# One retention-and-gated-MLP kernel on one core: every engine's instructions put into another order by a new table of numbers

## The chip, the cores and the metric

One core of one Trainium2 chip runs the kernel, in one launch. The metric is the device time of one execution in microseconds (us). A kernel is timed in several runs and their median is compared. Its one profiled execution gives the trace from which the rows below come. The five engines each take their instructions strictly in the order in which the program holds them: TensorE (PE, matmuls; PEld are its weight loads), VectorE (DVE), ScalarE (ACT), GpSimd (POOL) and SyncE (SP, which only starts DMAs).

## The reference

For four batches, eight heads, 768 tokens and head width 64, a linear attention with a decaying state is computed, and then a gated projection of its output:

```python
gamma = 1.0 - 2.0 ** (-5.0 - np.arange(H))
for t in range(S):
    state = gamma * state + outer(k[t], v[t])        # per batch and head
    y[t] = (1 / sqrt(D)) * q[t] @ state
x = y, heads side by side                            # (4, 768, 512)
gate = sigmoid(sum over k < 5 of conv_w[k] * x shifted by k)
out = (gate * (x @ w_val)) @ w_out                   # all float32
```

## The kernel before, in words

**Tiling.** The 768 tokens of each batch are cut into 6 chunks of 128, so there are 24 pairs of batch and chunk, numbered g = 0 to 23 with the batch running fastest; g = 4c + b. Each g has one loaded tile `att` (q, k and v; 1 MB from g = 4 on, 768 KB before), in a ring of four buffers: the load of one g (`load`, L198) cannot start before the block that used the buffer four places earlier is through. A load also waits for the fourth-last projection matmul that stands before it in the program (`hold`, L178).

**Attention.** The first four g are done with whole 128-token matmuls (`wide_scores` L263, `turn` L350, `wide_state` L338, `wide_y` L319). From g = 4 on one `block(g)` (L720) holds some 128 small matmuls: the output from this chunk's masked scores (`y_scores`, L360), the state updates (`state`, L240), the output from the state (`y_state`, L360), and the next chunk's scores (`scores`, L219). Around a block, DVE masks the scores (`mask`, L228, tile `u`), ACT copies the state out (`snap`, L250), POOL scales v by the decay (`decay`, L210, writing `att`), and DVE takes the result out to `x` (`evac`, L413).

**Projections.** For every token chunk n = 0 to 5 the four batches together are 512 columns. The value projection (`val(n, m, i)`, L555) is twelve matmuls for each of four column groups m; the output projection (`outp(n, b, i, cs)`, L583) is twelve for each batch b. Float32 precision is had by splitting: each operand is rounded (`xh`, `gvh`, `wvh`, `woh`, on ACT, L422, L571, L524) and its remainder is kept (`xl`, `gvl`, `wvl`, `wol`, on POOL, L426, L575, L528), and three products are summed. The twelve matmuls of one tile keep their order. Their order in `outp` is the one below, so the tenth, eleventh and twelfth need the fourth weight row block of w_out (number 7 of the eight blocks of both weights), rounded and remainder:

```python
ct = i // 3
gvh, gvl = gvs[n, ct]
gg, w = ((gvh, woh), (gvh, wol), (gvl, woh))[i % 3]
```

Results sit in two PSUM banks `mm` in turn; a bank comes free when DVE (`gated`, L564) or ACT (`store`, L593) has read it. The gate's convolution is one ACT and four DVE steps for each tile (`tap`, L539 and L541), then a sigmoid on ACT (L548).

**Weights.** The weights arrive as 64-bit words (`load_w`, L441: eight blocks, number 0 with the small tables as `first_sb`) and are turned into float32 on the chip, in a chain over three engines for each block n: three ACT steps (L465, L469, L473), `cv_bits`, `cv_top`, `cv_exp`, `cv_rest` on DVE (L484, L490, L496, L500), `cv_sum` (L507) on POOL, or on DVE for block 7, then `cv_round` on ACT (L524) and `cv_low` on POOL (L528).

**What sets the order.** Each piece of work is a `Step` with an engine, the tiles that it reads and writes, and a due time. `plan` (L49) sorts the steps by due time, which gives every step a number, and then issues them by the table `TURNS`, a list of those numbers; it only checks that the order respects data and buffers. Negative entries are fillers: -1 a 512-column and -2 a 128-column matmul of zeros (`fill`, L325) that keeps TensorE occupied. So the table alone decides, for each engine, what stands before what:

```python
for step in plan(steps, TURNS, [Step(0.0, "PE", 0.2345, [], [], fill, (n,)) for n in (512, 128)]):
    step.fn(*step.args)
```

Of the kernel before, what the change touches and what calls it, by code (L numbers as in the profile page):

```python
# [91 lines left out]
def tile_retention_gated_mlp(  # L92
# [507 lines left out]
    def first_sigmoid():  # L600
# [28 lines left out]
        12, 6, 5, 1, 2, 13, 11, 4, 0, 20, 15, 17, 14, 19, -2, 28, 8, 29, 7, 18, 10, 46, 59, 60, 21, 53,  # L629
        16, 70, 22, -2, -1, -2, -1, -1, 32, 81, 61, 62, 63, 64, 23, 65, 24, 66, 33, 9, 26, 25, 94, 35,  # L630
        -1, 48, 34, 36, 3, 95, 52, 27, 47, 96, 49, 97, 74, 136, 67, 51, 71, 75, 68, 50, 30, 98, 31, 82,
        69, 72, 99, 54, 116, 84, 100, 106, 55, 58, 79, 107, 101, 57, 108, 73, 83, 56, 109, 80, 78, 110,
        85, 102, 76, 103, 91, 77, 86, 87, 111, 89, 104, 37, 112, 90, 117, 88, 38, 154, 93, 113, 127, 92,
        125, 118, 146, 39, 199, 105, 133, 128, 126, 130, 119, 40, 137, 120, 42, 41, 140, 121, 132, 142,
        -1, 200, 43, 141, 131, 147, 201, 114, 122, 202, 148, 165, 149, 115, 139, 203, 150, 135, 123,
        166, 151, 153, 155, 134, 144, 171, 206, 167, 172, 145, 129, 168, 173, 174, 138, 169, 156, 152,
        -2, 209, 175, 214, 170, 211, 143, 158, 124, 161, 193, 212, 213, 44, 215, 176, 192, 197, 222,
        216, 191, 159, 160, 223, 157, 194, 219, 45, 162, 205, 224, 163, 177, 220, 238, 239, 207, 225,
        281, 178, 196, 282, 283, 195, 269, 198, 284, 240, 241, 204, 164, 244, 179, 287, 226, 246, 218,
        210, 270, 221, 227, 271, 181, 208, 182, 272, 255, 217, 288, 232, 183, 289, 180, 259, 290, 228,  # L640
        318, 260, 261, 184, 229, 262, 319, 263, 230, 316, 273, 231, 322, 185, 236, 274, 266, 248, 186,
        317, 233, 367, 249, 237, 368, 291, 243, 292, 264, 187, 320, 276, 293, 250, 242, 369, 295, 267,
        323, 251, 370, 360, 245, 247, 297, 321, 361, 252, 188, 362, 372, 253, 324, 296, 373, 268, 325,
        277, 374, 326, 254, 327, 328, 329, 275, 300, 256, 375, 376, 363, 377, 279, 378, 189, 330, 301,
        331, 234, 257, 379, 190, 332, 364, 278, 280, 302, 365, 258, 298, 381, 306, 303, 333, 299, 307,
        477, 343, 478, 479, 382, 480, 294, 481, 308, 334, 304, 482, 235, 335, 285, 339, 345, 483, 309,
        346, 348, 305, 310, 383, 336, 311, 371, 484, 385, 366, 398, 452, 399, 485, 312, 386, 400, 502,
        402, 384, 403, 404, 337, 405, 313, 406, 265, 387, 454, 314, 388, 455, 315, 486, 390, 338, 487,
        488, 456, 407, 489, 408, 409, 355, 504, 392, 410, 457, 340, 490, 286, 341, 411, 342, 344, 356,
        347, 380, 391, 349, 350, 413, 462, 463, 393, 464, 414, 458, 465, 351, 563, 352, 353, 354, 506,  # L650
        466, 565, 467, 397, 468, 395, 469, 470, 436, 471, 415, 357, 472, 358, 473, 416, 394, 474, 417,
        418, 419, 448, 420, 451, 434, 450, 401, 421, 460, 422, 423, 424, 425, 498, 426, 435, 427, 389,
        510, 437, 396, 475, 453, 412, 492, 476, 507, 428, 459, 500, 429, 430, 438, 439, 431, 511, 440,
        441, 493, 442, 432, 443, 444, 501, 461, 512, 433, 445, 513, 494, 446, 514, 447, 566, 515, 499,
        517, 519, 666, 567, 667, 668, 491, 669, 568, 670, 671, 672, 495, 673, 569, 516, 674, 675, 496,
        676, 677, 520, 678, 521, 522, 509, 523, 524, 503, 525, 644, 505, 497, 536, 526, 645, 527, 573,
        508, 574, 646, 575, 359, 576, 577, 679, 648, 578, 579, 449, 580, 518, 581, 582, 540, 689, 583,
        584, 543, 690, 545, 585, 546, 547, 529, 548, 586, 549, 550, 649, 553, 587, 554, 588, 589, 555,
        557, 590, 560, 591, 592, 687, 593, 594, 595, 596, 651, 597, 598, 652, 599, 653, 600, 654, 655,
        602, 656, 657, 658, 533, 659, 530, 608, 531, 660, 535, 661, 650, 662, 532, 663, 603, 541, 552,  # L660
        730, 609, 538, 610, 611, 731, 612, 613, 624, 695, 627, 732, 614, 629, 542, 696, 631, 604, 632,
        615, 664, 537, 616, 617, 633, 698, 528, 605, 634, 635, 636, 606, 639, 640, 699, 641, 618, 534,
        642, 619, 544, 607, 688, 680, 620, 681, 621, 539, 559, 700, 682, 637, 558, 736, 665, 737, 556,
        738, 701, 702, 733, 739, 703, 622, 704, 734, 705, 706, 707, 564, 709, 623, 710, 711, 683, 561,
        684, 685, 735, 740, 625, 807, 712, 741, 742, 713, 765, 743, 551, 744, 808, 745, 562, 714, 746,
        601, 792, 793, 715, 747, 794, 795, 748, 796, 797, 766, 799, 818, 819, 800, 767, 801, 802, 803,
# [388 lines left out]
```

## Time and profile before

| | us |
|---|---|
| median of three runs | 211.51 (210.23 to 211.98) |
| the profiled execution | 210.03 |
| its span, first to last instruction | 208.3 |

| engine | busy us | share of the span |
|---|---|---|
| PE | 199.1 | 96% |
| DVE | 136.2 | 65% |
| ACT | 110.3 | 53% |
| POOL | 105.8 | 51% |

The profiled execution is 1.7 us longer than its span, and 1.5 us shorter than the median of the runs. Matmuls are pipelined and overlap, so PE's busy time is not the sum of their durations; the step from one start to the next is what a matmul costs in a dense stretch.

### The profile page before, as it was taken

What the parts mean: (1) busy time and instruction counts of PE and PEld (TensorE: products, weight loads), DVE (VectorE), ACT (ScalarE), POOL (GpSimd) and SP (SyncE); (2) the same over time, 40 slices, a digit from 0 to 9 for tenths busy, and PEclk for the clock granted to TensorE, in tenths of its full rate; (3) what the DMA queues carried; (4) which work ended last, traced back from release to release, by engine and by line L of the source; (5) the groups of instructions that cost most, each with busy time, mean ns of one, the idle gap of its engine ahead of it and who ended that gap; (6) DMA issues with size and microseconds to landing.
All of it is one profiled execution on the core that took longest, in us unless ns stands there. A gap on an engine that the chain in (4) does not pass through costs nothing.

```text
span 208.3 us, 7483 instructions
## 1 busy us (share of the span) xinstructions
PE 199.1 (96%) x3317; PEld 160.4 (77%) x3317; DVE 136.2 (65%) x209; ACT 110.3 (53%) x228; POOL 105.8 (51%) x98
## 2 busy tenths in 40 slices
PE   3999699999999999999999999999999999999993
PEld 2688587786788788787788888788878787877783
DVE  0998999999999592956077888533956457671000
ACT  4577894797486745362665144737060753523321
POOL 2377699899884725934019620295420465132200
PEclk9999999999999999999999999999999999999999
DMA  6999988876463525928104663272010111111122
GB/s 205 389 407 341 344 325 337 307 302 209 127 233 157 178 80 200 385 82 296 53 3 149 260 168 140 89 270 99 9 50 0 50 53 50 50 50 50 50 104 101
DMA packets 8402, 35.18 MB, mean 169 GB/s; under 512 B 937, under 2 KB 1193, under 8 KB 5810
## 3 DMA queue, kind: packets, MB, share of 16 engines
q1 hardware_dynamic: 8352, 34.66, 45.4%
q8 instruction: 26, 0.43, 0.8%
q10 hardware_dynamic: 18, 0.04, 0.3%
q14 instruction: 6, 0.05, 0.1%
HBM read 28.41 MB, written 6.29 MB: 167 GB/s over the span
## 4 chain that ended last, share of the span: by engine, by line
PE 82%; DMA 7%; POOL 4%; ACT 3%; issue 1%; DVE 0%; ACTq 0%; POOLq 0%; SPq 0%
PE mm L583 32%; PE mm L555 29%; PE sy L360 9%; DMA att<-in_att_dram 6%; PE sy L219 4%; PE z_ps L240 3%; POOL xl L426 2%; POOL att L210 1%; PE sy L263 1%; DMA wst<-in_fall_dram 1%; PE mm L350 1%; PE z_ps L325 1%; ACT xh L422 1%; POOL wvl L528 1%; ACT snap L250 1%
## 5 line engine op out<-in xcount | busy, mean ns | idle before, releaser
L541 DVE SCALAR_TENSOR_TENSOR acc<-x,cw_sb,acc 128x512 f32<-128x512 f32 x96 | 70.4, 752 | 5.5 <-ACT acc L539 4.3
L575 POOL TENSOR_TENSOR gvl<-gate,gvh 128x512 fp32r<-128x512 f32 x24 | 31.0, 1296 | 45.9 <-ACT gvh L571 45.9
L426 POOL TENSOR_TENSOR xl<-x,xh 128x512 fp32r<-128x512 f32 x24 | 30.6, 1295 | 21.4 <-ACT xh L422 21.2
L583 PE MATMUL mm<-wol,gvh 128*128 128x512 f32 (+1 forms) x100 | 38.3, 387 | 0.0
L583 PE MATMUL mm<-woh,gvh 128*128 128x512 f32 (+1 forms) x100 | 38.3, 389 | 0.0
L564 DVE TENSOR_TENSOR gate<-mm,gate 128x512 f32<-128x512 f32 x24 | 16.5, 689 | 33.3 <-PE mm L555 20.7
L583 PE MATMUL mm<-woh,gvl 128*128 128x512 f32 (+1 forms) x100 | 38.0, 387 | 0.0
L593 ACT COPY o_sb<-mm 128x512 f32<-128x512 f32 (+1 forms) x25 | 14.2, 571 | 39.7 <-PE mm L583 39.6
L555 PE MATMUL mm<-xh,wvh 128*128 128x512 f32 x96 | 30.7, 408 | 0.3 <-ACT xh L422 0.2
L555 PE MATMUL mm<-xl,wvh 128*128 128x512 f32 x96 | 30.3, 399 | 0.1
L210 POOL TENSOR_TENSOR att<-att,first_sb 128x512 f32<-128x512 f32 x24 | 25.1, 1049 | 9.1 <-DMA att<-in_att_dram 5.6
L555 PE MATMUL mm<-xh,wvl 128*128 128x512 f32 x96 | 29.0, 400 | 0.0
L548 ACT ACTIVATE gate<-acc 128x512 f32<-128x512 f32 x24 | 14.3, 599 | 20.0 <-DVE acc L541 19.3
L583 PEld LDWEIGHTS mm<-woh,gvh 128*128 128x128 f32 x100 | 18.7, 188 | 5.3 <-ACT o_sb L593 1.6
L583 PEld LDWEIGHTS mm<-woh,gvl 128*128 128x128 f32 x100 | 18.8, 188 | 4.0
L583 PEld LDWEIGHTS mm<-wol,gvh 128*128 128x128 f32 x100 | 18.8, 188 | 3.9
L555 PEld LDWEIGHTS mm<-xl,wvh 128*128 128x128 f32 x96 | 17.9, 188 | 4.6 <-POOL xl L426 0.5
L555 PEld LDWEIGHTS mm<-xh,wvh 128*128 128x128 f32 x96 | 17.3, 188 | 5.0 <-ACT xh L422 0.9
L555 PEld LDWEIGHTS mm<-xh,wvl 128*128 128x128 f32 x96 | 17.9, 188 | 4.2
L571 ACT CAST gvh<-gate 128x512 fp32r<-128x512 f32 x24 | 14.8, 619 | 9.5 <-DVE gate L564 7.7
L250 ACT COPY snap<-z_ps 128x256 f32<-128x256 f32 x40 | 14.0, 374 | 9.1 <-PE z_ps L240 6.5
L539 ACT ACTIVATE acc<-x,cw_sb 128x512 f32<-128x512 f32 x24 | 16.5, 695 | 3.8 <-DVE rest L500 3.6
(65 smaller groups left out, 262.2 us busy)
## 6 DMA issues: line engine op xcount, KB each, us to landing
att<-in_att_dram SPq DMA_DIRECT2D x20, 1024.0 KB, 5.7
out_dram<-o_sb SPq DMA_DIRECT2D x23, 256.0 KB, 2.4
wst<-in_w_dram SPq DMA_DIRECT2D x7, 512.0 KB, 7.6
att<-in_att_dram SPq DMA_DIRECT2D x3, 768.0 KB, 8.1
first_sb<-in_first_dram SPq DMA_DIRECT2D x1, 568.0 KB, 4.0
att<-in_att_dram SPq DMA_DIRECT2D x1, 512.0 KB, 4.8
att<-in_att_dram SPq DMA_DIRECT2D x1, 256.0 KB, 8.3
out_dram<-o_sb SPq DMA_DIRECT2D x2, 128.0 KB, 1.8
```

The costliest lines, as they stand in the source:

```text
L210: nc.gpsimd.tensor_tensor(v, v, vd_sb[:, c, :].unsqueeze(2).broadcast_to([P, 8, HALF]), op=ALU.mult)
L250: nc.scalar.copy(sn, z_ps[:, :, b])
L360: return nc.tensor.matmul(sy[cols, h, off:off + HALF], lhsT=lhsT, rhs=rhs, start=start, stop=True, skip_group_check=True,)
L426: nc.gpsimd.tensor_tensor(xl[n, ct], xs[n][:, ct, :, HALO:], xh[n, ct].bitcast(F32), op=ALU.subtract)
L539: nc.scalar.mul(acc, x[:, :, 0:P], cw_sb[:, m, 0:1])
L541: nc.vector.scalar_tensor_tensor(acc, x[:, :, k:k + P], cw_sb[:, m, k:k + 1], acc, op0=ALU.mult, op1=ALU.add,)
L548: nc.scalar.activation(gate[n, m], accs.pop((n, m)), AF.Sigmoid)
L555: products.append(nc.tensor.matmul(vps[n, m], lhsT=w[:, m, ct * P:(ct + 1) * P], rhs=xx[n, ct].rearrange("p b t -> p (b t)"), start=(i == ...
L564: nc.vector.tensor_tensor(gv, vps.pop((n, m)), gv, op=ALU.mult)
L571: nc.scalar.copy(gvs[n, m][0], gate[n, m])
L575: nc.gpsimd.tensor_tensor(gvl, gate.pop((n, m)), gvh.bitcast(F32), op=ALU.subtract)
L583: products.append(nc.tensor.matmul(ops[n, b, cs.start][:, 0:cs.stop - cs.start], lhsT=gg[:, b * P:(b + 1) * P], rhs=w[:, ct, cs], start=(i ...
```

## The change

Only the table `TURNS` changes. The steps, their numbers, the buffers and the holds on loads are the same. The new table has 1219 entries for 1226: the five 512-column and four 128-column fillers become one of each, the 1217 steps are all kept, and the last 321 entries, from step 873 on, are the same in both. A line of the start of each:

```diff
     TURNS = (
-        12, 6, 5, 1, 2, 13, 11, 4, 0, 20, 15, 17, 14, 19, -2, 28, 8, 29, 7, 18, 10, 46, 59, 60, 21, 53,
-        16, 70, 22, -2, -1, -2, -1, -1, 32, 81, 61, 62, 63, 64, 23, 65, 24, 66, 33, 9, 26, 25, 94, 35,
...
+        12, 6, 1, 2, 13, 4, 0, 11, 5, 15, 3, 20, 14, 17, 19, 7, 8, 28, 9, 59, 18, 60, 16, 10, 29, 61,
+        46, 21, 32, 53, 62, 22, 70, 23, 63, 33, 24, 35, 26, 25, 48, 36, 34, 136, 64, 47, 65, 49, 27, 66,
...
```

**SyncE, the first loads.** The first rows after the branch, in the kernel before; a row's size is partitions by 4-byte words, `x2` stands for two alike:

```order
L436 DMA first_sb<-in_first_dram 128x1136
L198 DMA att<-in_att_dram 128x1024
L441 DMA wst<-in_w_dram 128x1024
L198 DMA att<-in_att_dram 128x1536 x2
L198 DMA att<-in_att_dram 128x512
L198 DMA att<-in_att_dram 128x1536
L441 DMA wst<-in_w_dram 128x1024 x2
```

and in the changed one:

```order
L436 DMA first_sb<-in_first_dram 128x1136
L198 DMA att<-in_att_dram 128x1024
L198 DMA att<-in_att_dram 128x1536
L441 DMA wst<-in_w_dram 128x1024
L198 DMA att<-in_att_dram 128x512
L198 DMA att<-in_att_dram 128x1536 x2
L441 DMA wst<-in_w_dram 128x1024 x2
```

The tile of g = 1 now goes third, ahead of weight block 1, and the v of g = 0 (the 512-word row) goes ahead of the tiles of g = 3 and 2. What stands before weight block 3 (the last row's first) is the same set in both. Further on, weight block 6 moves ahead of the load of g = 5, block 4 ahead of that of g = 7, and g = 9 ahead of g = 8.

**VectorE, the last weight block.** Between the mask of g = 11 and the first tap behind the sum of weight block 7, before (`u` is a mask, `gate<-mm` a gating, `x<-sy` an evacuation, `rest<-acc,top` the sum of block 7):

```order
L228 TENSOR_TENSOR u<-sy,tri_sb 128x512
L413 TENSOR_TENSOR x<-sy,dec 128x512
L541 SCALAR_TENSOR_TENSOR acc<-x,cw_sb,acc 128x512
L484 SCALAR_TENSOR_TENSOR acc<-wst,acc 128x512
L490 SCALAR_TENSOR_TENSOR top<-wst,acc 128x512
L564 TENSOR_TENSOR gate<-mm,gate 128x512
L496 TENSOR_SCALAR acc<-top 128x512
L413 TENSOR_TENSOR x<-sy,dec 128x512
L500 SCALAR_TENSOR_TENSOR acc<-wst,acc 128x512
L228 TENSOR_TENSOR u<-sy,tri_sb 128x512
L507 TENSOR_TENSOR rest<-acc,top 128x512
```

and in the changed kernel:

```order
L228 TENSOR_TENSOR u<-sy,tri_sb 128x512
L564 TENSOR_TENSOR gate<-mm,gate 128x512
L490 SCALAR_TENSOR_TENSOR top<-wst,acc 128x512
L413 TENSOR_TENSOR x<-sy,dec 128x512
L496 TENSOR_SCALAR acc<-top 128x512
L500 SCALAR_TENSOR_TENSOR acc<-wst,acc 128x512
L507 TENSOR_TENSOR rest<-acc,top 128x512
L228 TENSOR_TENSOR u<-sy,tri_sb 128x512
```

The evacuation of g = 11 and the mask of g = 12 now stand behind the sum, so two steps fewer are ahead of it; the two rows that are missing above moved ahead of the first.

**TensorE, between block 11 and block 12.** The output products of chunk 0 there, with tile numbers (before, `mm_1166` is batch 3 and `mm_1270` batch 1; gvh_1154 and gvl_1155 belong to the fourth row block):

```order
L583 MATMUL mm_1166<-wol_95,gvh_961 128x512
L583 MATMUL mm_1270<-woh_94,gvh_718 128x512
L583 MATMUL mm_1270<-wol_95,gvh_718 128x512
L583 MATMUL mm_1166<-woh_94,gvl_962 128x512
L583 MATMUL mm_1270<-woh_94,gvl_719 128x512
L583 MATMUL mm_1270<-woh_94,gvh_722 128x512
L583 MATMUL mm_1270<-wol_95,gvh_722 128x512
L583 MATMUL mm_1270<-woh_94,gvl_723 128x512
L583 MATMUL mm_1270<-woh_94,gvh_961 128x512
L583 MATMUL mm_1270<-wol_95,gvh_961 128x512
L360 MATMUL sy_97<-u_1283,att_1076 64x64 x16
```

and after (`mm_1164` is batch 3, `mm_1186` batch 1; gvh_1063 and gvl_1064 belong to the fourth row block), without the first five rows, which are batch 1's products of the second and third row blocks:

```order
L583 MATMUL mm_1186<-woh_94,gvl_958 128x512
L583 MATMUL mm_1186<-woh_94,gvh_1063 128x512
L583 MATMUL mm_1164<-woh_94,gvh_1063 128x512
L583 MATMUL mm_1164<-wol_95,gvh_1063 128x512
L583 MATMUL mm_1164<-woh_94,gvl_1064 128x512
L583 MATMUL mm_1186<-wol_95,gvh_1063 128x512
L583 MATMUL mm_1186<-woh_94,gvl_1064 128x512
L360 MATMUL sy_97<-u_1262,att_1044 64x64 x16
```

The products of the fourth row block, for which weight block 7 must be ready, moved from behind block 12 to ahead of it.

## Rows read from the trace of the kernel before

**Rows 1.** Busy time of each engine in two stretches (us, PE, PEld, DVE, ACT, POOL, PEclk, DMA).

```profile
core 0: us, PE busy (x) PEld busy (x) DVE busy (x) ACT busy (x) POOL busy (x), PEclk, DMA share, GB/s
22.00:57.00 35.00, 32.92 (x914) 25.79 (x910) 34.48 (x56) 25.91 (x56) 31.98 (x27) 1.00 0.75 279
57.00:205.00 148.00, 147.76 (x2187) 119.69 (x2179) 86.06 (x127) 70.08 (x143) 62.04 (x52) 1.00 0.34 120
```

**Rows 2.** Timeline of PE: first product, block 10, two products, the last one.

```profile
22.92 0.73 PE L555 MATMUL mm<-xh,wvh 128*128 128x512 f32 x2 [0.22 <-ACT xh L422]
...
56.59 0.69 PE L360 MATMUL sy<-u,att 64*64 64x64 f32 x32
...
58.61 0.50 PE L555 MATMUL mm<-xl,wvh 128*128 128x512 f32 x1
...
59.41 0.39 PE L583 MATMUL mm<-woh,gvl 128*128 128x512 f32 x1
59.64 0.39 PE L583 MATMUL mm<-woh,gvh 128*128 128x512 f32 x1
...
204.66 0.27 PE L583 MATMUL mm<-woh,gvl 128*128 128x256 f32 x1
```

**Rows 3.** Waits of PE and PEld, 22 to 57 us: total, times, longest.

```profile
PEld sy L360 <- DVE u L228: 1.5, 4, 0.4
PE z_ps L240 <- POOL att L210: 1.2, 3, 0.7
PEld z_ps L240 <- ACT snap L250: 0.9, 2, 0.5
PEld mm L555 <- POOL xl L426: 0.5, 1, 0.5
```

**Rows 4.** Timeline of PE in the first 13 us.

```profile
5.09 1.67 PE L325 MATMUL z_ps<-const-float32-0.0 128*128 128x128 bf16 x5
6.69 2.08 PE L263 MATMUL sy<-att 64*128 64x128 f32 x16
8.70 1.11 PE L350 MATMUL mm<-eye_sb,att 128*128 128x128 f32 x4
...
10.79 1.16 PE L263 MATMUL sy<-att 64*128 64x128 f32 x16
11.88 0.66 PE L350 MATMUL mm<-eye_sb,att 128*128 128x128 f32 x4
```

**Rows 5.** Timeline: weight block 3 reaches ACT and then DVE.

```profile
15.68 0.66 ACT L465 ACTIVATE acc<-wst 128x512 f32<-128x512 f32 x1 [0.72 <-DMA wst<-in_w_dram]
...
17.68 0.70 DVE L484 SCALAR_TENSOR_TENSOR acc<-wst,acc 128x512 int32<-128x512 int32 x1 [0.71 <-ACT acc L473]
```

**Rows 6.** Timeline of DVE up to the sum of weight block 7.

```profile
63.41 0.68 DVE L413 TENSOR_TENSOR x<-sy,dec 128x512 f32<-128x512 f32 x1
64.00 0.68 DVE L500 SCALAR_TENSOR_TENSOR acc<-wst,acc 128x512 f32<-128x512 uint16 x1
64.60 0.68 DVE L228 TENSOR_TENSOR u<-sy,tri_sb 128x512 f32<-128x512 f32 x1
65.20 0.68 DVE L507 TENSOR_TENSOR rest<-acc,top 128x512 f32<-128x512 f32 x1
```

**Rows 7.** Timeline of ACT and POOL: weight block 7 rounded, its remainder.

```profile
65.92 0.62 ACT L524 CAST woh<-rest 128x512 fp32r<-128x512 f32 x1 [0.34 <-DVE rest L507]
...
66.61 1.27 POOL L528 TENSOR_TENSOR wol<-rest,woh 128x512 fp32r<-128x512 f32 x1 [2.81 <-ACT woh L524]
```

**Rows 8.** Timeline of PE: block 12, the products behind it, and block 11's start.

```profile
61.12 0.69 PE L360 MATMUL sy<-u,att 64*64 64x64 f32 x32
...
65.68 0.69 PE L360 MATMUL sy<-u,att 64*64 64x64 f32 x32
...
67.70 0.50 PE L583 MATMUL mm<-woh,gvh 128*128 128x512 f32 x1
68.03 0.41 PE L583 MATMUL mm<-wol,gvh 128*128 128x512 f32 x1
```

**Rows 9.** Timeline of POOL: sum of block 5, remainders of blocks 4 and 5.

```profile
54.48 1.30 POOL L507 TENSOR_TENSOR rest<-rest,top 128x512 f32<-128x512 f32 x1 [0.29 <-DVE rest L500]
56.03 2.53 POOL L528 TENSOR_TENSOR wol<-rest,woh 128x512 fp32r<-128x512 f32 x2 [0.25 <-ACT woh L524]
```

**Rows 10.** Costliest groups of instructions: two of POOL (busy us, mean ns, idle before).

```profile
L575 POOL TENSOR_TENSOR gvl<-gate,gvh 128x512 fp32r<-128x512 f32 x24 | 31.0, 1296 | 45.9 <-ACT gvh L571 45.9
...
L210 POOL TENSOR_TENSOR att<-att,first_sb 128x512 f32<-128x512 f32 x24 | 25.1, 1049 | 9.1 <-DMA att<-in_att_dram 5.6
```

128 rows, old and new, of the table TURNS are left out of this document.

## The prediction, written before the changed kernel had run

> **What bounds the kernel now.** I read first the busy time by stretches [rows 1]. From 57 to 205 us TensorE is busy 147.76 of 148 us: behind 57 us nothing that another engine does can be seen on it, and every step on TensorE simply stands behind the one before. From 22 to 57 us it is VectorE that has no room (34.48 of 35 us), and GpSimd is nearly full too (31.98). So the end of the kernel is set by how much TensorE has done when it becomes dense, and that is set by VectorE and GpSimd.
>
> Next the timeline of TensorE [rows 2]. A product costs 0.23 us (59.41 to 59.64) and a block 2.02 us (56.59 to 58.61). From 22.92 to the start of block 10 at 56.59 the table puts 69 products and six blocks: 69 x 0.23 + 6 x 2.02 = 28.0 us of work in 33.7 us. Some 5.7 us are lost there, and the waits say for what [rows 3]: masks from VectorE, decayed values and remainders from GpSimd, state copies from ScalarE, each a few tenths. A new order can win only from these 5.7 us, from the start before 22.92 us, and nothing from the last matmul at 204.66 us on, since the last 321 entries of the table are the same.
>
> **The start.** Two things change there. The fillers: five ran at 5.09 us for 1.67 us [rows 4], and the first scores came behind them, at 6.69 us; the new table starts the scores as soon as their tile lands. And the loads: the tile of g = 1 goes third and the v of g = 0 comes earlier, so the buffer of g = 0 should come free earlier and with it the load of g = 4. Neither reaches VectorE's full stretch. That one begins with weight block 3: ScalarE waited 0.72 us for its landing (15.68 us), and VectorE 0.71 us for ScalarE (17.68 us) [rows 5]. The same bytes stand ahead of block 3 in both orders, so it lands at the same time, and the same three ScalarE steps (15.68 to 17.68) follow. I take 0 for the start. The bounds: 0.7 us better, VectorE's wait gone, if block 3 lands earlier; 1.5 us worse by the clock (the first rival).
>
> **Weight block 7 and the point where TensorE gets dense.** The longest chain that the new table puts in front of TensorE is that of the last weight block. Before, TensorE reached its remainder behind block 12: the product with `wol` at 68.03 us [rows 8], with the remainder ready at 66.61 + 1.27 = 67.88 us [rows 7], so 0.15 us of room. In the new order the two products with `wol` of row block 7 stand ahead of block 12. What is ready by then can be counted in the table: at the first of these products TensorE has behind it 72 value products, 20 output products and the blocks up to 11. Before, at the start of block 12 (65.68 us [rows 8]) it had the same with 17 output products, so the same amount of work was done at 65.68 + 3 x 0.23 = 66.37 us. That is the mark: the remainder of block 7 before 66.37 us is a gain, behind it a loss, one for one, as all the work that follows is the same and was dense.
>
> When is it ready? The sum of block 7 on VectorE started at 65.20 and took 0.68 [rows 6]. Two steps that stood before it, an evacuation and a mask, now stand behind it; from start to start they took 0.59 us (63.41 to 64.00) and 0.60 us (64.60 to 65.20), together 1.19. The rounding on ScalarE and the remainder on GpSimd follow as before: from the sum's end at 65.88 to 67.88, 2.00 us [rows 6, 7]. At VectorE's old pace that is 65.88 - 1.19 + 2.00 = 66.69 us, 0.32 us late. VectorE was idle 0.52 us between 22 and 57 us [rows 1]; the new order has masks and sums in other places, where I find their inputs earlier, so I give it 0.5 us of that (bounds 0 and 0.5, plus the 0.7 of the start). Then the remainder is there at 66.19 us, and the gain is 0.18 us.
>
> **Does TensorE get there in time?** The three more products by block 10 (72 for 69) and five more by block 11 are work in hand, some 1 us of it, which pays for the waits that the order has anew. The dearest is weight block 5. Its remainder came 4.10 us behind the start of its sum (54.48 to 56.03 + 2.53 = 58.56 us [rows 9]). The new order puts a decay (1.05 us) and a remainder of the gated values (1.30 us) ahead of it [rows 10], and so 6.45 us. At the old pace this is 60.93 us; VectorE's step before the sum stands one place (0.60 us) earlier, and with the 0.5 us from above it is 59.83 us. From there eight products, block 11 and eight products lead to the first product with block 7: 59.83 + 16 x 0.23 + 2.02 = 65.5 us, before 66.19. At the old pace it would be 66.6 us, so this second chain nearly binds as well: 0.2 us late at worst. Hence I take it as hidden; without the cover it costs that 0.2.
>
> **Behind 67 us** the order is new as well up to about 155 us. There TensorE had no wait to lose and VectorE, ScalarE and GpSimd were busy 86, 70 and 62 of 148 us [rows 1], so every new wait is a pure loss and none a gain. I went through the buffers: a decay for g = 21 stands on GpSimd ahead of two remainders of chunk 2, and its load behind a store and the load of g = 19; there some 3 us of room are left by the count of products. I take 0, with 3 us as the upper bound, when one load is late by twice that room.
>
> **Sum.** Start 0, block 7 -0.18, the rest 0: about -0.2 us. The profiled execution of 210.03 us would become 209.8, and the median of the runs, 211.51, 211.3 us. (The profiled one is 1.5 us faster than the median; I forecast the median.)
>
> **Rivals.** (1) The clock at the start; slower. The PEclk column reads 1.00, yet the first sixteen score matmuls took 2.08 us at 6.69 us and the next sixteen 1.16 us at 10.79; four transposes 1.11 and then 0.66 [rows 4]. So TensorE ran at its lower level, 1.2 GHz, until about 10.5 us, and at 2.4 GHz behind. Until then it had been kept occupied from 3.6 us on, by fillers where there was no work. Without them it stands still for about a microsecond before the first scores. If the rise comes later by the second scores, a state and an output (0.92 us for the scores, about as much for the other two together), part of it hides behind the wait for the tile of g = 2 and some 1.5 us reach VectorE. Then block 7 is ready at 67.7 us, 1.3 us behind the mark: 212.8 us. It decides from the point where VectorE's step of block 3 starts later than 17.9 us. Against it: the engine is at work without a pause from about 6.2 us on. The Trainium skill speaks for it (TensorE: Matmul & The Clock Gate, Part 1: The HAM clock gate): the slow clock is the resting state, and only sustained activity lifts it; by that rule alone the missing fillers put the rise off, and the sum would be this rival's.
>
> (2) A new wait behind 67 us, in a stretch that is dense now; 1 to 3 us, so 212.5 to 214.5. For it: everything is reordered and nothing can be won there. Against it: two thirds of the time of VectorE and half of that of the others is free.
>
> (3) Block 7 stops binding. If the loads at the start come earlier by VectorE's 0.71 us of waiting [rows 5] and the 0.5 us hold, the remainder is ready at 65.5 us, when TensorE arrives: a gain of 0.9 us, 210.6. With the waits of the middle shorter too, 2 us: 209.5. For it: 5.7 us are lost in the middle, and the new order does have more products in hand. Against it: VectorE's list up to the sum is the same list less two steps, and it was full.
>
> (4) It does nothing at all: the work of all engines is the same and TensorE's is 96% of the span; then the time is 211.5, which differs from the forecast by less than can be told.
>
> **How the numbers follow.** Forecast and (4), which a measurement cannot part: 0.56. Rival (1) 0.14, (2) 0.12, (3) 0.18. Faster or slower by over 1% means under 209.4 or over 213.6 us, which is about what a measurement of this kernel can tell from no change. Under 209.4 lie half of (3) and a little of the forecast: 0.13. Over 213.6 lie most of (2) and the bad end of (1), with a stall that I did not see: 0.18. The rest, 0.69, is within 1%. The likeliest case alone has 210.6 to 212.1. The range 209.3 to 213.6 leaves out about 1 in 10 on either side.
>
> **What would show it.** Right: VectorE's first step on block 3 within 0.3 us of 17.68; the sum of block 7 ending near 64.2 us; TensorE waiting for `wol` ahead of block 12 and starting that block near 67.1 us, with four more products than the 20 behind it; nothing but tenths of waits behind it. Wrong: sixteen scores at 2 us each still behind 11 us; a gap on TensorE behind 70 us; or block 12 started without a wait.

## The result and the profile after

The changed kernel takes 212.43 us (median of 20 runs, 211.19 to 214.04), the kernel before 211.54 us (20 runs alternating with them, 209.99 to 213.71): 1.0065 of the time before, 95% interval 1.0044 to 1.0086. It is slower, by 0.9 us, where 0.2 us of gain was forecast; the time lies inside the range and within 1%.

The profiled executions lie further apart than the medians: 211.71 us after, 210.03 before. That of before was near the fast end of its runs. Ratios of many runs decide below, and single traces show where a delay sits. A ratio leaves out executions over 1.5% above the fastest of their kernel, so it can differ from the ratio of two medians (run 10 in the table below).

The busy time by stretches of the changed kernel, to be held against [rows 1]:

```profile
core 0: us, PE busy (x) PEld busy (x) DVE busy (x) ACT busy (x) POOL busy (x), PEclk, DMA share, GB/s
22.00:57.00 35.00, 33.95 (x926) 26.50 (x923) 34.52 (x55) 25.86 (x54) 31.55 (x28) 1.00 0.73 267
57.00:205.00 148.00, 147.06 (x2188) 118.41 (x2187) 86.42 (x129) 70.15 (x144) 63.81 (x53) 1.00 0.35 121
```

VectorE is as full from 22 to 57 us as before. Behind 57 us TensorE is idle for 0.94 us in place of 0.24, nearly all of it at block 10 (shown with run 5). Its last matmul, for which [rows 2] have 204.66 us:

```profile
206.38 0.27 PE L583 MATMUL mm<-woh,gvl 128*128 128x256 f32 x1
```

Now the start, on the timeline of TensorE (start, duration, instruction, output and inputs, count, idle time before it and what ended that), against [rows 4]:

```profile
6.10 2.08 PE L263 MATMUL sy<-att 64*128 64x128 f32 x16 [0.92 <-DMA att<-in_att_dram]
8.11 1.11 PE L350 MATMUL mm<-eye_sb,att 128*128 128x128 f32 x4
9.64 1.09 PE L350 MATMUL mm<-eye_sb,att 128*128 128x128 f32 x4 [0.42 <-DMA att<-in_att_dram]
10.65 2.08 PE L263 MATMUL sy<-att 64*128 64x128 f32 x16
```

The second sixteen scores still take 2.08 us (1.16 before): TensorE is at its lower level, 1.2 GHz, behind 10.5 us, though the PEclk column reads 1.00 there as well. Then weight block 3 on ScalarE and VectorE, against [rows 5]:

```profile
16.54 0.67 ACT L465 ACTIVATE acc<-wst 128x512 f32<-128x512 f32 x1 [0.28 <-DMA wst<-in_w_dram]
...
18.54 0.70 DVE L484 SCALAR_TENSOR_TENSOR acc<-wst,acc 128x512 int32<-128x512 int32 x1 [0.49 <-ACT acc L473]
```

Both 0.86 us later than before. And the stretch of weight block 7: its sum on VectorE, its remainder on GpSimd, TensorE at the first product that needs it, and block 12 (against [rows 6 to 8]):

```profile
65.02 0.69 DVE L507 TENSOR_TENSOR rest<-acc,top 128x512 f32<-128x512 f32 x1
...
66.45 1.32 POOL L528 TENSOR_TENSOR wol<-rest,woh 128x512 fp32r<-128x512 f32 x1 [3.75 <-ACT woh L524]
...
67.97 0.40 PE L583 MATMUL mm<-wol,gvh 128*128 128x512 f32 x1
...
68.99 0.69 PE L360 MATMUL sy<-u,att 64*64 64x64 f32 x32
```

The remainder is ready at 67.77 us, and TensorE comes for it at 67.97, without a wait. The prediction's mark for that same point of work was 66.37 us. So TensorE is 1.6 us late there, nearly all of the 1.7 us by which its last matmul is late: the loss is made ahead of 68 us, and weight block 7 does not make it, though by 0.2 us only: had TensorE come earlier than that, it would have waited.

### The profile page after: what moved, and what is told of

The parts are those of the page before. It is cut to its first block, busy times and chain, and to the rows that moved or that the text cites. A ratio compares the mean times of both kernels' runs of the same rounds, so it can differ in the third digit from the quotient of the medians.

```text
span 210.0 us, 7467 instructions
## 1 busy us (share of the span) xinstructions
PE 199.4 (95%) x3310; PEld 160.2 (76%) x3310; DVE 135.7 (65%) x209; ACT 110.6 (53%) x228; POOL 105.5 (50%) x98
## 4 chain that ended last, share of the span: by engine, by line
PE 77%; POOL 6%; DMA 5%; DVE 4%; ACT 4%; issue 2%; SPq 0%; ACTq 0%
PE mm L583 32%; PE mm L555 25%; PE sy L360 7%; DMA att<-in_att_dram 5%; PE sy L219 3%; PE z_ps L240 3%; POOL xl L426 3%; PE sy L263 2%; DVE acc L541 2%; PE mm L319 1%; POOL rest L507 1%; PE z_ps L338 1%; PE mm L350 1%; POOL att L210 1%; ACT acc L465 1%
## 5 line engine op out<-in xcount | busy, mean ns | idle before, releaser
L541 DVE SCALAR_TENSOR_TENSOR acc<-x,cw_sb,acc 128x512 f32<-128x512 f32 x96 | 69.4, 750 | 10.4 <-ACT acc L539 9.4
L555 PE MATMUL mm<-xh,wvh 128*128 128x512 f32 x96 | 31.7, 410 | 0.3 <-ACT xh L422 0.2
L555 PE MATMUL mm<-xl,wvh 128*128 128x512 f32 x96 | 29.6, 400 | 0.1
L228 DVE TENSOR_TENSOR u<-sy,tri_sb 128x512 f32<-128x512 f32 x20 | 13.7, 684 | 7.6 <-PE sy L219 7.5
```

Source lines behind the costliest of these rows:

```text
L541: nc.vector.scalar_tensor_tensor(acc, x[:, :, k:k + P], cw_sb[:, m, k:k + 1], acc, op0=ALU.mult, op1=ALU.add,)
L555: products.append(nc.tensor.matmul(vps[n, m], lhsT=w[:, m, ct * P:(ct + 1) * P], rhs=xx[n, ct].rearrange("p b t -> p (b t)"), start=(i == ...
```

## The experiments

The eighteen kernels differ from the two known ones in the table alone (step numbers in the diffs; 20 is the load of weight block 1, 15 the tile of g = 1, 7 and 8 the position sums, 32 and 48 the first scores and the second transposes). Each was timed in five rounds beside the kernel before; ratios are to that kernel, with 95% intervals. "Changed" means the changed kernel.

### The start: fillers and third load (runs 1 to 4, 8)

Run 1, the fillers back in the changed kernel:

```diff
-17, 19, 7, 8, ... 21, 32, 53, ... 25, 48, 36, ...
+17, 19, -2, 7, 8, ... 21, -2, -1, -2, -1, -1, 32, 53, ... 25, -1, 48, 36, ...
```

> The changed order with the seven early fillers of the kernel before put back at their old places (one 128 ahead of the first matmul; 128, 512, 128, 512, 512 ahead of the first scores; 512 between the two transposes). Theory C (clock): the changed kernel ran its second sixteen scores at 2.08 us because TensorE's clock rose at 14.1 us and not at 10.5; with the fillers the rise is back near 10.5 us, the second scores take 1.16 us, and the time falls from 1.0065 of before to about 0.998. Theory L (third load): weight block 3 still reaches ScalarE at 16.5 us, VectorE's step on it still starts near 18.4 us, and the time stays near 1.005. Theory W (the wait for weight block 7 ahead of block 12 costs by itself): unchanged at 1.0065.

Measured 212.53 us, 1.0062 (1.0033 to 1.0092). The second scores run fast again, yet VectorE comes as late:

```profile
10.48 1.16 PE L263 MATMUL sy<-att 64*128 64x128 f32 x16
...
16.50 0.67 ACT L465 ACTIVATE acc<-wst 128x512 f32<-128x512 f32 x1 [1.84 <-DMA wst<-in_w_dram]
...
18.51 0.70 DVE L484 SCALAR_TENSOR_TENSOR acc<-wst,acc 128x512 int32<-128x512 int32 x1 [0.69 <-ACT acc L473]
```

ScalarE now stands 1.84 us for the landing: the loads alone hold it.

Run 2, weight block 1 third again, no fillers:

```diff
-0, 11, 5, 15, 3, 20, 14,
+0, 11, 5, 20, 15, 3, 14,
```

> The changed order with one load moved: weight block 1 third and the tile of g = 1 fourth, as before. Theory L: weight block 3 lands 0.9 us earlier, ScalarE starts on it at 15.7 us instead of 16.5, and the time falls to about 1.000. Theory C: the clock still rises near 14 us, ScalarE is held by the slow third transpose until 16.2 us anyway, so VectorE's step on block 3 moves by 0.3 us at most and the time stays at 1.005. Theory W: 1.0065.

Measured 213.02 us, 1.0111 (1.0064 to 1.0157). Here the load is in time and the clock is late:

```profile
10.97 2.08 PE L263 MATMUL sy<-att 64*128 64x128 f32 x16
...
16.87 0.64 ACT L465 ACTIVATE acc<-wst 128x512 f32<-128x512 f32 x1
...
18.85 0.70 DVE L484 SCALAR_TENSOR_TENSOR acc<-wst,acc 128x512 int32<-128x512 int32 x1
```

No landing is named ahead of ScalarE's step: its other work, which hangs on TensorE, came late. In these two traces either cause alone makes VectorE 0.8 to 1.2 us late at block 3.

Run 3 has both edits.

> Both: fillers back and weight block 1 third, the rest of the changed order kept. Theories C and L together: VectorE's step on block 3 starts at 17.7 us or earlier as before, the remainder of block 7 is ready near 66.3 us, and the time is 0.998 to 1.000 of before. Theory W: still 1.005 or more, with TensorE waiting ahead of block 12.

VectorE starts block 3 early again, so the start is repaired:

```profile
17.52 0.70 DVE L484 SCALAR_TENSOR_TENSOR acc<-wst,acc 128x512 int32<-128x512 int32 x1 [0.16 <-ACT acc L473]
```

But the time is 212.28 us, 1.0056 (1.0021 to 1.0091): hardly anything comes back. Its profiled execution took 215.8 us, so its trace is not read behind 52 us.

Run 4 takes the first seven fillers out of the kernel before.

```diff
-19, -2, 28, 8, ... 22, -2, -1, -2, -1, -1, 32, ... -1, 48, ...
+19, 28, 8, ... 22, 32, ... 48, ...
```

> The order before without its first seven fillers, nothing else. Theory C: the clock rises near 14 us here too, the second scores take 2.08 us, and the time rises to 1.004 to 1.007 of before. Theory L: the clock does not matter, VectorE's step on block 3 stays at 17.7 us and the time within 0.2% of before. Theory W: no change.

Measured 212.96 us, 1.0084 (1.0046 to 1.0121). So the fillers are worth something; but in this trace the second scores took 1.16 us and VectorE came at 17.95, and the loss that it shows is a wait of GpSimd, 1.73 us ahead of a decay at 36.20. By which path the median loses 0.8% is not shown. The sum over all traces helps with the clock: in the ten with these fillers (before among them) the second scores always took 1.16 us, in the ten without them 2.08 us three times (changed, runs 2 and 6), 1.48 and 1.20 once each, and 1.16 five times. Without fillers the clock's rise is late in some executions only.

Run 8 exchanges the third and the fourth load in the kernel before.

```diff
-0, 20, 15, 17, 14, 19,
+0, 15, 20, 17, 14, 19,
```

> The kernel before with one edit: the tile of g=1 (768 KB) third and weight block 1 (512 KB) fourth, its fillers kept. Theory S in its form L (a larger third load makes every byte behind it late): weight block 3 reaches ScalarE near 16.5 for 15.7, VectorE near 18.5 for 17.7, and the end is 0.8 to 0.9 us later, 212.4 us. If the start's delay is lost in waits that are there anyway: 211.6. If the order of the two loads does not matter to the arrival of block 3: 211.6 with VectorE at 17.7.

Measured 211.46 us beside 210.96, 1.0026 (0.9995 to 1.0057), VectorE at 18.45 us: the arrival as theory L has it, about half its price, with an interval that still holds no change. What the exchange does is seen in the answers on DMA for the third and the fourth load (size, us from issue to landing), before:

```profile
wst<-in_w_dram SPq DMA_DIRECT2D x1, 512.0 KB, 6.1
...
att<-in_att_dram SPq DMA_DIRECT2D x1, 768.0 KB, 6.6
```

and in the changed kernel:

```profile
att<-in_att_dram SPq DMA_DIRECT2D x1, 768.0 KB, 7.8
...
wst<-in_w_dram SPq DMA_DIRECT2D x1, 512.0 KB, 7.6
```

SyncE issues the fourth at 3.16 and 3.22 us, so the same 1.25 MB is in at 9.8 us before and 10.8 after; in run 8, with the exchange alone, at 10.2 (3.11 + 7.1). On the mean it is in at 9.8 us with weight block 1 third (10 traces, 9.5 to 10.2) and at 10.4 with g = 1 third (10 traces, 10.1 to 10.8). Over the traces VectorE starts block 3 at 17.7 us on the mean with weight block 1 third and the fillers in (8 traces, 17.47 to 18.02), at 18.3 with g = 1 third (10 traces, eight of them without the fillers, 17.80 to 18.62): 0.6 us, less than the 0.86 of the first two traces.

### Blocks 10 to 12 (runs 5 to 7)

The trace of the changed kernel has two waits on TensorE at block 10 that the kernel before has not:

```profile
58.47 0.69 PE L360 MATMUL sy<-u,att 64*64 64x64 f32 x32 [0.58 <-DVE x L413]
59.43 0.69 PE L240 MATMUL z_ps<-att 64*64 64x64 f32 x32 [0.26 <-ACT snap L250]
```

Run 5 takes both away: evacuations of g = 9 (275) and 10 (294) on VectorE and the state copy of g = 11 (279) on ScalarE earlier.

```diff
-277, 300, 331, 375, 363, ... 302, 278, 379, 365, 275, ... 303, 279, 280, ... 343, ... 398, 294, 399,
+277, 300, 279, 331, 375, 275, 363, ... 302, 278, 379, 365, ... 303, 280, ... 343, 294, ... 398, 399,
```

> After, with three moves between blocks 9 and 11: on VectorE the evacuation of g=9 ahead of the tap (1,1,3) and the evacuation of g=10 right behind the mask of g=11, on ScalarE the state copy of g=11 right behind the tap (1,0,0); all three as the kernel before has them. Theory M (a second loss, apart from the start: in the changed kernel TensorE waits 0.58 us ahead of block 10 for VectorE's evacuation and 0.26 us inside it for the state copy, and VectorE is held up behind it): block 10 starts at 57.9 for 58.47 with neither wait, 0.84 us come back, 211.7 us. Theory W (the wait for weight block 7 ahead of block 12 is just hidden by those 0.84 us): the product that needs it is reached near 67.1 while the remainder is ready near 67.8 to 68.4, so 0 to 0.2 us come back, 212.3 to 212.5. Theory S (all of the loss is the start's 0.86 us, from the third load and the clock): 212.5.

Measured 213.0 us, 1.0107 (1.0067 to 1.0147): nothing gained. Block 10 starts at 57.38 us without a wait, and half a microsecond is lost inside it instead, for GpSimd's decay:

```profile
58.82 0.46 PE L240 MATMUL z_ps<-att 64*64 64x64 f32 x16 [0.50 <-POOL att L210]
```

From block 4 to block 11 it takes 38.29 us (25.44 to 63.73), the changed kernel 38.26 (25.72 to 63.98).

Run 6 also puts the products that hang on block 7's remainder (486 to 488, 409, 410) and the store 489 behind block 12 (387).

```diff
-..., 486, ... 487, ... 488, ... 409, ... 489, 410, ... 387,
+..., 387, 486, 487, 488, 489, 409, 410,
```

> The run before with one more edit: the five output products of chunk 0 that read the fourth row block's remainder or follow such a one (batch 3's last three, batch 1's last two) stand behind block 12 instead of ahead of it, as in the kernel before. Theory M with W: the 0.84 us come back, 211.7 us, and no wait for POOL's wol stands ahead of block 12. Theory M without W: the same time as the run before, 211.7. Theory S: 212.5.

Measured 214.26 us, 1.0168 (1.0138 to 1.0199), the worst of all. Without these five products TensorE is at block 12 before VectorE has taken out g = 11:

```profile
69.74 0.69 PE L360 MATMUL sy<-u,att 64*64 64x64 f32 x32 [1.04 <-DVE x L413]
```

So the products that the prediction took for the trouble were what covered VectorE's later evacuation. Theory M falls, and so does W as a cost of its own: neither in the trace of the changed kernel nor in that of run 5 does TensorE stand for that remainder.

Run 7 repairs the start on top.

> The run before with the start repaired as well: the seven early fillers at their old places and weight block 1 as third load with the tile of g=1 fourth. Theories S and M together (two losses that add up): 212.5 - 0.86 - 0.84 = 210.8 us, VectorE at weight block 3 near 17.6, block 12 near 67. S alone: 211.6. M alone, the start worth nothing: 211.7. Neither: 212.3, as the changed kernel with its start repaired.

213.8 us, 1.0148 (1.0115 to 1.018): still bad, and again the early start gave back next to nothing.

### Cut and joined orders (runs 9 to 13, 16)

Since parts depend on one another, whole stretches were exchanged: the head of one table, then all remaining steps in the order of the other (fillers of the second that stood ahead of the cut left out).

```diff
-TURNS = AFTER
+TURNS = BEFORE[:120] + [s for s in AFTER if s not in BEFORE[:120]]
```

That is run 9. Runs 10 (AFTER[:115], then BEFORE), 11 and 16 (BEFORE[:263], then AFTER), 12 (AFTER[:382], then BEFORE) and 13 (AFTER[:115], then BEFORE as far as its entry 263, then AFTER) are made alike.

> The first 120 entries of the table of the kernel before (all that stands ahead of the first product (0,0,0), some 23 us, with its fillers and its loads), and behind them every other step in the order of the changed kernel. Theory S (the loss of 0.9 us sits in the start): as the kernel before, 211.5 us, and VectorE on block 3 near 17.7. Theory Mid (it sits in the order between 23 and 68 us): as the changed kernel, 212.4, with VectorE early at block 3 all the same. Theory Late (it sits behind 68 us): 212.4 too.

> The counterpart: the first 115 entries of the changed table (all ahead of its first product), then every other step in the order of the kernel before. Theory S: 212.4 us, VectorE on block 3 near 18.5 and block 12 near 66.5. Theories Mid and Late: 211.5 us, the late start lost in waits that are there anyway.

> The order of the kernel before as far as block 8 (entry 263, some 45 us), behind it that of the changed kernel. Theory S: 211.5 us. Theory Mid in its early half (23 to 45 us): 211.5. Theory Mid in its late half (45 to 68 us, where TensorE waits 0.58 us for the evacuation of g=9 and 0.26 us for a state copy): 212.4, block 10 waiting for VectorE. Theory Late: 212.4.

> The order of the changed kernel as far as the load of g=16 ahead of block 12 (entry 382, some 68 us), behind it that of the kernel before. Theories S and Mid: as the changed kernel, 212.4 us. Theory Late: 211.5. With the run before it this tells whether anything behind 68 us costs or gives back.

> The changed kernel with one stretch in the order of the kernel before: the first 115 entries (up to its first product) are the changed ones, from there to block 8 (some 23 to 45 us) stand the steps in the order of the kernel before, behind that again the changed order. Beside the hybrid with the start of before as well (210.93 us) it measures the start by itself. Theory 'start and 23-45 us are two delays that run beside each other and do not add up': 211.4 us (0.4 to 0.5 us, as the start alone cost in the order of before). Theory 'only 23-45 us costs': 210.9. Theory 'only the start': 212.4.

> The hybrid that keeps the order of before to block 8 and the changed order behind it, once more, since it came out at 0.9976 of the kernel before with an interval that just reaches 1. If its late part gives something back (as exchanging it for that of before cost the changed kernel 0.6%): 0.995 to 0.998 again, 210.5 to 211.1 us. If it was chance: 0.999 to 1.002.

| run | to 23 us | 23 to 45 us | behind 45 us | us | ratio to before |
|---|---|---|---|---|---|
| 11 | before | before | changed | 210.93 | 0.9976 (0.9951 to 1.0002) |
| 16 | before | before | changed | 211.03 | 0.9979 (0.9949 to 1.0009) |
| 9 | before | changed | changed | 212.44 | 1.0070 (1.0038 to 1.0102) |
| 13 | changed | before | changed | 212.17 | 1.0034 (1.0000 to 1.0069) |
| changed kernel | changed | changed | changed | 212.43 | 1.0065 (1.0044 to 1.0086) |
| 10 | changed | before | before | 212.71 | 1.0042 (1.0013 to 1.0072) |
| 12 | changed | changed | changed to 68 us, then before | 213.97 | 1.0125 (1.0096 to 1.0153) |

Four readings. The changed stretch from 23 to 45 us costs 0.9% by itself (9 less 11; run 3, which has the start repaired and no joint at 23 us, less 11 gives 0.8%). The changed start costs 0.4 to 0.6% by itself (10; 13 less 16). Together they cost 0.9% (changed kernel less 11), not the sum of some 1.4: they lie beside each other, which is why repairing the start alone (runs 3, 9) gave nothing. Each of these differences is uncertain by 0.3 to 0.5%, so that they do not add is likely and not certain. Run 13 alone, 212.17 us, lies nearer to what was expected for "only the start" (212.4) than for two delays (211.4); it is run 9 that rules the former out. And the changed order behind 45 us costs nothing: runs 11 and 16 are at 0.998 both, each interval just reaching 1. Theory Late falls.

Run 12 is slower than either time that was expected for it (212.4 or 211.5 us) and 0.6% slower than the changed kernel. Its trace tells of the joint and not of the order behind 68 us, since TensorE waits at block 12 for VectorE's evacuation and then for GpSimd's decay:

```profile
67.87 0.69 PE L360 MATMUL sy<-u,att 64*64 64x64 f32 x32 [0.48 <-DVE x L413]
...
69.75 0.46 PE L240 MATMUL z_ps<-att 64*64 64x64 f32 x16 [0.95 <-POOL att L210]
```

At the joint that decay (68.65 us) has come to stand behind two remainders on GpSimd (66.17 and 67.42 us). In the kernel before it stands ahead of both (62.76), in the changed kernel directly behind the first (67.71). So a cut can cost something that neither table costs by itself. The kernel of runs 11 and 16 is the fastest here, 0.2% under the kernel before, which is not certain.

### What it is between 23 and 45 us (runs 14, 15, 17, 18)

In the trace of run 9 four engines pass a delay on. Rows of GpSimd (decay of g = 8), ScalarE (a sigmoid, then weight block 4's first step) and VectorE (block 4's first step):

```profile
40.68 1.04 POOL L210 TENSOR_TENSOR att<-att,first_sb 128x512 f32<-128x512 f32 x1 [1.33 <-DMA att<-in_att_dram]
41.68 2.53 POOL L575 TENSOR_TENSOR gvl<-gate,gvh 128x512 fp32r<-128x512 f32 x2
...
42.99 0.60 ACT L548 ACTIVATE gate<-acc 128x512 f32<-128x512 f32 x1 [1.49 <-POOL gvl L575]
43.62 0.65 ACT L465 ACTIVATE acc<-wst 128x512 f32<-128x512 f32 x1
...
45.60 0.70 DVE L484 SCALAR_TENSOR_TENSOR acc<-wst,acc 128x512 int32<-128x512 int32 x1 [0.53 <-ACT acc L473]
```

GpSimd waits for the load of g = 8, which the changed table issues behind that of g = 9, here at 33.21 us, for 28.74 in the kernel before. Two remainders stand behind that decay, the sigmoid waits for the first of them, block 4 stands behind the sigmoid, and VectorE waits. In the changed kernel's own trace that load landed in 5.9 us, in time; in run 9's it took 7.3, in those of runs 1 and 6 7.0 and 7.6. A second suspect: the sigmoid also needs the tap (0,2,4), which now stands behind (0,3,1).

Run 14 is run 9 with the two taps exchanged, run 15 the changed kernel with the same.

```diff
-270, 246, 230, 288, 210, 226, 221, 271,
+226, 270, 246, 230, 288, 210, 221, 271,
```

> The hybrid with the start of before and all else changed (212.44 us), with two neighbouring taps on VectorE exchanged: the tap (0,2,4) ahead of (0,3,1), as in the kernel before. Theory A (ScalarE holds VectorE at 45 us: its sigmoid 0,2 waits 1.49 us for that tap and weight block 4's three steps stand behind it, so VectorE waits 0.53 us ahead of block 4's first step and the repaired start is lost there): that wait goes, VectorE is 0.5 us earlier at the mask of g=9 (49.3 for 49.85), 211.9 us. Theory B (the loss lies at blocks 4 and 5, where TensorE waits 0.96 us for a state copy and 0.46 us for the evacuation of g=4): 212.4.

> The changed kernel with the same two taps exchanged and nothing else. In its trace the wait ahead of block 4's first step is only 0.08 us, since VectorE comes as late by itself. Theory 'two delays beside each other': 212.4 us, nothing gained without the start. If it falls to 212 or below, the late start is not what holds VectorE there.

Run 14: 211.71 us, 1.0011 (0.9976 to 1.0045), so 0.6% of run 9's 0.9% is gone, and VectorE's wait at weight block 4 with it. But in that trace the load of g = 8 was earlier too, and the sigmoid stood for GpSimd's remainder again (1.09 us), not for the tap. Run 15: 212.0 us, 1.0031 (1.0000 to 1.0061), which is better than expected, within the uncertainty of the changed kernel, and by the sign named beforehand (212 or below) speaks against the late start as what holds VectorE there. But in its trace the tap was no help, since the sigmoid stood 1.66 us until GpSimd's remainder:

```profile
40.50 1.05 POOL L210 TENSOR_TENSOR att<-att,first_sb 128x512 f32<-128x512 f32 x1 [1.48 <-DMA att<-in_att_dram]
...
42.82 0.60 ACT L548 ACTIVATE gate<-acc 128x512 f32<-128x512 f32 x1 [1.66 <-POOL gvl L575]
...
45.43 0.69 DVE L484 SCALAR_TENSOR_TENSOR acc<-wst,acc 128x512 int32<-128x512 int32 x1 [0.56 <-ACT acc L473]
```

Run 17 is run 9 with the loads of g = 8 (135) and 9 (152) exchanged, run 18 the changed kernel with that.

```diff
-148, 115, 152, 200, ... 135, ...
+148, 115, 135, 200, ... 152, ...
```

> The hybrid with the start of before and all else changed (212.44 us), with two loads exchanged: the load of g=8 at the place of that of g=9, and g=9 at its place, so that g=8 is again loaded first, as in the kernel before. Theory D (the late load of g=8 is the second delay: issued at 33.2 instead of 28.7 us it lands between 39.2 and 41.0 from run to run, POOL's decay of g=8 waits up to 1.5 us for it, the two remainders behind that decay release ScalarE's sigmoid 0,2, weight block 4's three steps stand behind it, and VectorE waits 0.5 us for these): no wait for a DMA in POOL near 40 us, the sigmoid starts with the tap's end near 42.4 for 42.99, VectorE at the mask of g=9 near 49.3 for 49.85, 211.9 us. Theory A alone (the order of the two taps is the cause): 212.4, as the tap still ends at 42.4 and the rest is unchanged.

> The changed kernel with the same two loads exchanged and nothing else. Its own trace showed no wait for the load of g=8 (it landed at 39.35, before POOL came), five traces of its variants showed 0.9 to 1.6 us. Theory D: the executions in which the load lands late lose that, 0.2 to 0.5 us of the median: 211.9 to 212.2 us, and no wait for a DMA in POOL near 40 us. If start and load were one and the same delay, or the load only follows it: 212.4.

Run 17's trace is as theory D drew it, no wait for a DMA, the sigmoid at 42.39 us, no wait at weight block 4:

```profile
39.18 1.05 POOL L210 TENSOR_TENSOR att<-att,first_sb 128x512 f32<-128x512 f32 x1
...
42.39 0.60 ACT L548 ACTIVATE gate<-acc 128x512 f32<-128x512 f32 x1 [1.03 <-DVE acc L541]
...
45.01 0.70 DVE L484 SCALAR_TENSOR_TENSOR acc<-wst,acc 128x512 int32<-128x512 int32 x1
```

but its time is 212.14 us, 1.0062 (1.0039 to 1.0085), as good as run 9's 1.0070. Run 18: 211.76 us, 1.0041 (1.0018 to 1.0063). So the late load is a wait that is real in single executions and not the whole 0.9%; neither suspect is. With one of the two exchanges, the other suspect still holds the sigmoid in each of these four traces (the tap for 1.03 us in run 17); both exchanges at once were not tried.

One sign is common to all thirteen traces with the changed stretch, and missing in the three timed with that stretch as before and the changed order behind it (11, 13, 16). TensorE, between block 8 and block 9, in the changed kernel:

```profile
46.84 0.69 PE L360 MATMUL sy<-u,att 64*64 64x64 f32 x32
...
48.86 1.73 PE L555 MATMUL mm<-xh,wvh 128*128 128x512 f32 x6
50.82 0.51 PE L555 MATMUL mm<-xh,wvh 128*128 128x512 f32 x1 [0.23 <-ACT xh L422]
```

and in run 16:

```profile
46.42 0.69 PE L360 MATMUL sy<-u,att 64*64 64x64 f32 x32
...
48.44 1.89 PE L555 MATMUL mm<-xh,wvh 128*128 128x512 f32 x7
50.17 0.39 PE L555 MATMUL mm<-xh,wvl 128*128 128x512 f32 x1
50.40 0.39 PE L555 MATMUL mm<-xh,wvh 128*128 128x512 f32 x1
50.63 0.40 PE L555 MATMUL mm<-xh,wvl 128*128 128x512 f32 x1
50.96 0.69 PE L360 MATMUL sy<-u,att 64*64 64x64 f32 x32
```

Ten products lie between these blocks in either. Run 16 takes 4.54 us from block to block; the changed kernel reaches block 9 at 51.95, after 5.11. ScalarE has one rounding of x more to do there, which the order of before has done by 44.6 us; the next one, for which TensorE waits 0.23 us, is 1.1 us later for it. Over the traces it is 5.09 to 5.80 us in the thirteen and 4.54 to 4.59 in the three, so 0.5 us or more of TensorE's time goes there. Run 14 has it too (5.17 us), at a time of 1.0011, so it is not the whole cost either. Moving that one rounding alone was not tried, so how the 0.9% divides between the rounding, the load, the taps and TensorE's waits at attention blocks 4 and 5 (theory B of run 14) stays open.

## Why the prediction was wrong

**The start, taken as 0.** The step that failed is "The same bytes stand ahead of block 3 in both orders, so it lands at the same time". The bytes were the same, the landing was not: with 768 KB as third load in place of 512 KB the first 1.25 MB behind the second load were in 1.0 us later, and block 3 reached VectorE 0.86 us late in the trace; on the mean of many both were 0.6 us late. Why the same bytes take longer in that order is not shown. My bounds for the start (0.7 better, 1.5 worse) held it, and the price, 0.4 to 0.6% or 0.9 to 1.2 us, is that of a term that I had put at 0.

**Rival (1), the clock.** Its mechanism was in the trace, by its own sign: scores at 2.08 us behind 10.5 us, and VectorE's step behind its 17.9 us (18.54). Its price of 1.3 us was above the 0.9 measured. But run 1 shows that the fillers alone bring nothing back, as the loads hold the same step; and the traces show the late rise in three of ten executions without fillers, not in all. The Trainium skill (TensorE: Matmul & The Clock Gate, Part 1: The HAM clock gate) says that the number of slow matmuls differs from run to run of one kernel; the traces agree: in the eight kernels that share the changed start the second scores took 1.16 us four times, 1.20 and 1.48 once each and 2.08 twice. I weighed that rival as if it happened always or never.

**Weight block 7, taken as -0.18.** The step that failed is "Then the remainder is there at 66.19 us": it was there at 67.77. I had the sum end near 64.2 us, by taking two steps off VectorE's list and 0.5 us out of its idle time; it ended at 65.71, as the 0.86 us of the start stood in front and no idle time came back. The rule of the mark, a loss "one for one", was not put to the test: the remainder lay 1.4 us behind the mark of 66.37, but TensorE lay 1.6 us behind it for other reasons, so nothing stood for block 7. It was close everywhere. In twelve traces (changed, runs 1, 2, 5, 9, 11 and 13 to 18) the remainder is ready between 66.56 and 69.32 us, and TensorE comes for it 0.06 to 0.38 us later. It is closest in runs 11, 13 and 16, here run 16:

```profile
65.26 1.30 POOL L528 TENSOR_TENSOR wol<-rest,woh 128x512 fp32r<-128x512 f32 x1 [4.23 <-ACT woh L524]
...
66.63 0.48 PE L583 MATMUL mm<-wol,gvh 128*128 128x512 f32 x1
```

So as long as the remainder came no earlier, TensorE's own waits ahead of it could give back no more than these tenths; that both keep the pace of VectorE is the likely reason, and not tested. Run 6 shows that taking its products away from there costs 1.3 us more. The evacuation, which I counted as merely moved behind the sum, is what block 12 waits for (1.04 us in run 6).

**23 to 45 us, taken as a reservoir of 5.7 us that could only be won from.** Only a few terms there were priced: VectorE's list, and weight block 5 on GpSimd. The 0.9% of this stretch was no term of the sum. What I had in hand: the front shows that the load of g = 9 goes ahead of that of g = 8, and I did not follow it to the decay that waits for it; nor did I look for roundings on ScalarE that moved from one side of a block to the other. Full engines hide such losses: VectorE was 34.5 of 35 us busy before and after.

**Behind 67 us, taken as 0.** Right. From the same point of work to the last matmul TensorE takes 138.41 us (67.97 to 206.38), for 138.29 before (66.37, the mark, to 204.66). Rival (2) did not happen, nor rival (3).

**The signs named beforehand.** VectorE at block 3 within 0.3 us of 17.68: missed by 0.86. The sum of block 7 ending near 64.2: 65.71. TensorE waiting for `wol` ahead of block 12, and that near 67.1: no wait, 68.99. "Sixteen scores at 2 us each still behind 11 us" and "block 12 started without a wait" were named as signs of an error, and both are there.

## What to carry to other kernels

Two delays beside each other need not add, so undoing one can show nothing: when a repair that works in the trace leaves the time where it was, cut the program in stretches and exchange these, and only then look for the single step. Look for waits at the joint first, since neither program has them (run 12). Equal bytes ahead of a transfer do not mean equal arrival; look at the size of what is queued while the first issues are slow. A stall that comes in some executions only (a load that lands in 5.9 or 7.6 us, a clock that rises at once or later) is missing from one trace and present in the median, so read the same row in several.

## What the hardware did that was not expected

In 18 of the 20 traces SyncE takes 1.1 to 1.5 us for its third issue, be it 512 or 768 KB, while the second and the fourth take 0.4 to 0.6; in runs 13 and 14 the third takes 0.4 us and the fourth 1.0 and 1.2. With the larger load third the two loads behind the second were in 0.6 us later on the mean, with the DMA engines' busy share from 2 to 10 us above 0.9 both in the kernel before and in the changed one.

A tap on VectorE that stands directly behind the one whose result it needs starts 0.78 us after it (25.58 to 26.36 us in the changed kernel), other steps of that size 0.60 to 0.66 us apart. So four taps of two tiles take 2.86 us where one such pair is among them, in run 9:

```profile
41.02 2.86 DVE L541 SCALAR_TENSOR_TENSOR acc<-x,cw_sb,acc 128x512 f32<-128x512 f32 x4
```

and 2.99 us with two such pairs, in run 14:

```profile
40.58 2.99 DVE L541 SCALAR_TENSOR_TENSOR acc<-x,cw_sb,acc 128x512 f32<-128x512 f32 x4
```

The exchange of the taps has a price of its own, 0.13 us, that the expectation of run 14 left out.
